# Attention scores of two heads as two 64-row matmuls of 128 queries, in a new order of steps

## The chip, the core and the metric

The program runs on one core of a Trainium2 chip. The number that counts is the device time of one execution in microseconds (us), as a median of several runs. TensorE is called PE here (PEld is its weight load), VectorE DVE, ScalarE ACT, GpSimd POOL, and SyncE, which issues most of the DMAs, SP.

## What is computed

The program does three things one after the other: attention with a causal mask and a bias from a running sum, a mixture of eight experts, and a gated layer. Only the attention is touched:

```python
batch, n_heads, seq, head_dim = (4, 8, 576, 64)
scores = scale * np.matmul(q, k.transpose(0, 1, 3, 2))
s_pos = np.maximum(s, 0.0)
cum = np.cumsum(s_pos, axis=-1)
bias = -(cum[:, :, :, None] - cum[:, :, None, :])
scores = np.where(causal, -1000000000.0, scores + np.minimum(bias, 0.0))
scores = scores - np.max(scores, axis=-1, keepdims=True)
attn = np.exp(scores)
attn = attn / (np.sum(attn, axis=-1, keepdims=True) + 1e-09)
return np.matmul(attn, v).astype(np.float32)
```

Since every row's maximum is subtracted, a constant per row falls out, so only the running sum of the keys has to be added to the scores.

## The kernel before

The 32 heads are worked on as 16 pairs p = 0..15; a pair's two heads lie in partitions 0 to 63 and 64 to 127 of q, k and v. One pair goes through these steps:

- `attn_load`, `load_bias`, `load_v` (L212 to L238): DMAs of q, k, the running sum from a scratch tensor `cumd`, broadcast over 64 partitions per head, and v. `q_diag` (L241, POOL) spreads q into nine block-diagonal tiles `bd` of 128 x 128: head 0's 64 queries in one quarter, head 1's in the opposite one, zeros elsewhere.
- `s_mm` i = 0..8 (L255): 64 queries of both heads against w = 64(i+1) keys, one matmul over all 128 rows (L266), then a bf16 matmul over the last 64 columns that adds the mask (L268). DVE adds the running sum and takes the row's minimum (L269) into one of three `sc` buffers. i = 8 is done in two halves of 288 columns.
- `s_exp` i = 0..8 (L276): ACT takes the exponential and sums it up (L279). `s_norm` (L283): DVE gathers the sums of both heads and takes reciprocals.
- `t_mm` g = 0..6 (L295): 25 transposes of 128 x 128, four to a PSUM bank (L302), each bank copied by ACT (L304).
- `pv_mm` j = 0..4 (L307): attention times v; the two heads write partitions 0 to 63 and 64 to 127 of one bank (L318, L322). `pv_out` (ACT) copies out.
- `o_mm` i = 0..4 (L333): transposes back with the router's weights appended (L346); DVE scales by the reciprocals (L350, L353).
- After every fourth pair `route` (L370) picks the experts in a chain of small DVE steps with one group of matmuls in it (L409 to L413), and scatters rows to memory.

An f32 matmul is two MATMUL instructions (two passes) with a weight load each. On PE, ACT and DVE the order is the program's: `attention` (L524) adds every step to a list at 10p + a position from the table `POS` and sorts, so that steps of several pairs interleave; T of one pair runs among S of the next, for example. POOL's order and that of the DMA issues on SP are the framework's. PSUM has eight banks, which all of these steps take in turn.

At the start `cumulate` (L127) makes the running sum on DVE, writes it to `cumd`, and for pair 0 alone spreads it over partitions with matmuls (L145).

Of the kernel before, what the change touches and what calls it, by code (L numbers as in the profile page):

```python
# [89 lines left out]
def masks(k):  # L90
    nc, P = k.nc, k.apool
    k.identb = P.tile([128, 128], BF16, name="identb")
    nc.vector.tensor_copy(k.identb, k.ident)
    mk = slot(k, 8, [128], name="mk")
    k.maskm = P.tile([128, 64], BF16, name="maskm")
# [3 lines left out]
    nc.vector.tensor_copy(k.maskm[0:64, :], mk[0:64, 0:64])  # L99
    nc.vector.tensor_copy(k.maskm[64:128, :], mk[64:128, 64:128])  # L100


# [24 lines left out]
def cumulate(k):  # L127
    nc = k.nc
    w = slot(k, 7, [3 * S + NBIAS], name="cumw")[0:32, :]
    s, z, c, d = w[:, 0:S], w[:, S:2 * S], w[:, 2 * S:3 * S], w[:, 3 * S:]  # L130
# [8 lines left out]
    both = k.apool.tile([32, 128], F32, name="both")  # L139
    nc.vector.tensor_copy(both.rearrange("p (h n) -> p h n", h=2),  # L140
                          k.ident[0:32, 0:2].unsqueeze(2).broadcast_to((32, 2, 64)))
    yield
    for n, (a, b) in enumerate(((0, 256), (256, 768), (768, 1280), (1280, 1344))):
        ps = k.psum.tile([128, 512], F32, name=f"cb{n}", tag="b")
        nc.tensor.matmul(ps[:, 0:b - a], both, d[:, a:b], start=True, stop=True)  # L145
        nc.scalar.copy(k.st[0].bias[:, a:b], ps[:, 0:b - a])
        yield

# [24 lines left out]
NBIAS = 1344  # L173
BASE = (0, 0, 0, 0, 256, 256, 256, 256, 768)
NT64 = S // 64
PB = (0, 1, 2, 4, 6, 9, 12, 16, 20)
JB = (0, 9, 16, 21, 24)
NBLK = 25
BLOCKS = [(j, i) for j in range(5) for i in range(2 * j, NT64)]
HALF = S // 2  # L180


def attn_statics(k):
    nc, A = k.nc, k.apool
    k.inp, k.p, k.pvt = [], [], []
    for n in range(2):
        w = slot(k, 4 + n, [3648], name=f"in{n}")
        bd = w[:, 2496:3648].rearrange("p (i n) -> p i n", n=128)
        nc.gpsimd.memset(bd[0:64, :, 64:128], 0.0)
        nc.gpsimd.memset(bd[64:128, :, 0:64], 0.0)  # L190
        k.inp.append((w[:, 0:576], w[:, 576:1152], w[:, 1152:2496], bd))
        if n == 0:
            attn_load(k, 0)
    w = slot(k, 3, [3200], name="vp")
    k.vv = [w[:, 640 * n:640 * n + 640].rearrange("p (h j d) -> p h j d", h=2, j=5) for n in range(3)]
    k.pvt = [w[:, 1920 + 640 * n:2560 + 640 * n] for n in range(2)]
    for n in range(2):
        nc.gpsimd.memset(k.pvt[n][:, S:640], 0.0)
        p = slot(k, n, [NBLK * 128], name=f"p{n}")
        for i in range(0, NT64, 2):  # L200
            nc.gpsimd.memset(p[:, 128 * PB[i] + 64 * (i + 1):128 * PB[i] + 64 * (i + 2)], 0.0)
        k.p.append(p)
    k.pt = slot(k, 2, [NBLK * 128], name="pt")
# [89 lines left out]


def t_mm(k, p, g):  # L295
    nc = k.nc
    src = k.p[p % 2]
    ps = k.psum.tile([128, 512], F32, name=f"t{p}_{g}", tag="b")
    blocks = BLOCKS[4 * g:4 * g + 4]
    for n, (j, i) in enumerate(blocks):  # L300
        a = 128 * (PB[i] + j)
        nc.tensor.transpose(ps[:, 128 * n:128 * n + 128], src[:, a:a + 128], k.ident)  # L302
    w = 128 * len(blocks)
    nc.scalar.copy(k.pt[:, 512 * g:512 * g + w], ps[:, 0:w])  # L304


def pv_mm(k, p, j):  # L307
    nc = k.nc
    st = k.st[p]
    pt = k.pt.rearrange("p (b h n) -> p b h n", h=2, n=64)  # L310
# [141 lines left out]
def order_experts(k):  # L452
# [71 lines left out]
def attention(k):  # L524
    k.st, k.todo = {}, []
    with ExitStack() as es:
# [23 lines left out]
        for p in range(NP):  # L550
# [707 lines left out]
def block_kernel(ctx, tc, q, kk, v, s, w_gate, w1, w2, wg, wv, wo, rms_g, out):  # L1258
# [8 lines left out]
    k.cumd = k.dpool.tile([32, NBIAS], F32, name="cumd")  # L1267
# [80 lines left out]
```

## Time and profile before

| | |
|---|---|
| median of 3 runs | 947.14 us (945.52 to 948.28) |
| the profiled execution | 944.19 us, of which 942.5 us is the span from first to last instruction |
| PE busy | 904.4 us (96%), 5560 matmul instructions |
| DVE / ACT / POOL busy | 463.1 / 407.7 / 346.3 us |

Matmuls overlap in their pipeline, so a matmul's own duration is longer than the step from its start to the next one's start; what a matmul costs PE is that step. The shares of the whole span are means over very different stages; the attention lies in about the first 224 us.

### The profile page before, as it was taken

How to read it: one execution, taken by the hardware profiler on the slowest of the kernel's cores; microseconds unless marked ns; L12 is line 12 of the kernel's file. 1: busy time of each engine (PE TensorE's matmuls, PEld its weight loads, DVE VectorE, ACT ScalarE, POOL GpSimd, SP SyncE). 2: the span in 40 equal slices, each digit the busy share in tenths (PEclk: the TensorE clock that was granted, in tenths of full speed). 3: DMA queues.
4: the chain of work that ended last, by engine and by line, in shares of the span. 5: the costliest groups of instructions: out<-in, count | busy, mean ns of one | idle time of the engine just before them, and what ended most of it. 6: DMA issues, size and time to landing. Idle time of an engine off the chain costs nothing.

```text
span 942.5 us, 15470 instructions
## 1 busy us (share of the span) xinstructions
PE 904.4 (96%) x5560; PEld 800.5 (85%) x5560; DVE 463.1 (49%) x1368; ACT 407.7 (43%) x963; POOL 346.3 (37%) x324
## 2 busy tenths in 40 slices
PE   6999999999979999999899999999999998899995
PEld 3677777678869999999899999999999995688884
DVE  4556565555442555335795444555444699800000
ACT  3777777776546565566351111111111222333310
POOL 4102333124447666767111011110011146697541
PEclk9999999999989999999999999999999999999998
DMA  6986675431637656565731111101111122110000
GB/s 203 276 248 177 165 215 165 110 101 51 211 117 219 208 186 176 185 190 163 244 111 45 46 45 45 45 26 43 46 45 45 46 90 90 47 68 34 34 34 37
DMA packets 47658, 109.13 MB, mean 116 GB/s; under 512 B 6688, under 2 KB 14395, under 8 KB 47571
## 3 DMA queue, kind: packets, MB, share of 16 engines
q1 hardware_dynamic: 44611, 98.42, 35.0%
q0 software_dynamic: 2912, 9.46, 2.6%
q8 instruction: 45, 0.74, 0.3%
q14 instruction: 42, 0.34, 0.1%
q10 hardware_dynamic: 48, 0.17, 0.0%
HBM read 87.17 MB, written 20.86 MB: 115 GB/s over the span
## 4 chain that ended last, share of the span: by engine, by line
PE 83%; DVE 8%; issue 4%; POOL 2%; ACT 1%; POOLq 0%; ACTq 0%; DVEq 0%
PE gg L1028 32%; PE g L750 11%; PE s L266 9%; PE g L734 8%; PE go L1053 8%; PE pvy L318 5%; PE t L302 4%; PE tl L346 3%; DVE raw L981 2%; DVE raw L971 1%; PE xp L705 1%; PE r L799 1%; ACT raw L975 1%; PE r L788 1%; PE cb L145 1%
## 5 line engine op out<-in xcount | busy, mean ns | idle before, releaser
L1028 PE MATMUL gg<-gx,ws 128*128 128x384 f32 x1728 | 300.4, 335 | 0.0
L1028 PEld LDWEIGHTS gg<-gx,ws 128*128 128x128 f32 x1728 | 299.6, 188 | 0.1
L618 POOL TENSOR_TENSOR u<-raw,u 128x1024 fp32r<-128x1024 f32 x64 | 153.9, 2418 | 105.8 <-ACT u L617 102.1
L984 POOL TENSOR_TENSOR ws<-raw,ws 128x256 fp32r<-128x256 f32 x48 | 36.7, 785 | 257.5 <-DVE ws L983 250.3
L269 DVE CUSTOM_DVE_ANT_0 sc<-s,in 128x288 f32<-128x288 f32 (+8 forms) x160 | 70.5, 452 | 85.6 <-PE s L268 78.9
L750 PE MATMUL g<-h,u 128*128 128x256 f32 (+7 forms) x768 | 107.3, 298 | 4.5 <-DVE h L738 3.3
L750 PEld LDWEIGHTS g<-h,u 128*128 128x128 f32 x768 | 102.9, 191 | 5.6 <-DVE h L738 3.7
L266 PE MATMUL s<-in 128*128 128x288 f32 (+8 forms) x320 | 105.2, 429 | 0.1
L734 PE MATMUL g<-xt,u 128*128 128x256 f32 (+7 forms) x768 | 104.2, 295 | 0.0
L734 PEld LDWEIGHTS g<-xt,u 128*128 128x128 f32 x768 | 101.4, 188 | 0.8
L1034 ACT ACTIVATE gh<-gg 128x384 f32<-128x384 f32 x72 | 35.3, 491 | 152.5 <-PE gg L1028 152.5
L279 ACT ACTIVATE p<-sc,nm 128x64 f32<-128x64 f32 (+2 forms) x144 | 81.0, 563 | 14.5 <-DVE nm L272 8.1
L975 ACT ACTIVATE raw<-raw 128x256 f32<-128x256 f32 x72 | 28.0, 440 | 124.4 <-DVE raw L973 117.3
L1035 DVE TENSOR_TENSOR gh<-gg,gh 128x384 f32<-128x384 f32 x72 | 39.9, 555 | 74.5 <-ACT gh L1034 74.5
L617 ACT CAST u<-raw 128x1024 fp32r<-128x1024 f32 x64 | 67.0, 1047 | 4.2 <-DMA raw<-in_w 4.2
L304 ACT COPY pt<-t 128x512 f32<-128x512 f32 (+1 forms) x112 | 59.6, 536 | 19.2 <-PE t L302 18.6
L243 POOL COPY in<-in 64x576 f32<-64x576 f32 x30 | 20.2, 673 | 117.4 <-PE s L268 50.6
L302 PE MATMUL t<-ident,p 128*128 128x128 f32 x400 | 63.1, 276 | 0.0
L1036 DVE TENSOR_TENSOR gh<-gg,gh 128x384 f32<-128x384 f32 x72 | 40.2, 558 | 44.8 <-PE gg L1028 41.3
L758 DVE TENSOR_TENSOR sq<-sq,sn 128x256 f32<-128x256 f32 (+7 forms) x24 | 15.5, 646 | 87.4 <-ACT sn L757 87.4
L266 PEld LDWEIGHTS s<-in 128*128 128x128 f32 x320 | 50.6, 196 | 5.0 <-issue 0.8
L302 PEld LDWEIGHTS t<-ident,p 128*128 128x128 f32 x400 | 46.3, 141 | 2.3 <-DVE nm L269 0.5
(227 smaller groups left out, 1211.7 us busy)
## 6 DMA issues: line engine op xcount, KB each, us to landing
raw<-in_w SPq DMA_DIRECT2D x64, 512.0 KB
in<-cumd SPq DMA_DIRECT2D x30, 336.0 KB
xs<-zrow SPq DMA_DIRECT2D x8, 771.0 KB
raw<-in_wg SPq DMA_DIRECT2D x24, 256.0 KB
raw<-in_wv SPq DMA_DIRECT2D x24, 256.0 KB
raw<-in_wo SPq DMA_DIRECT2D x24, 256.0 KB
vp<-in_v SPq DMA_DIRECT2D x16, 320.0 KB
in<-in_k SPq DMA_DIRECT2D x16, 288.0 KB
```

The source lines that it names most:

```text
L266: nc.tensor.matmul(ps, st.bd[:, i, :], st.k[:, a:b], start=True, stop=not last)
L269: nc.vector.tensor_tensor_reduce(out=sc[:, a:b], in0=ps, in1=st.bias[:, BASE[i] + a:BASE[i] + b], scale=-0.125, scalar=3e38, op0=ALU.add, ...
L279: k.nc.scalar.activation(k.p[p % 2][:, 128 * PB[i]:128 * PB[i] + w], st.p[i][:, 0:w], AF.Exp, bias=st.nm[:, i:i + 1], scale=-1.0, accum_ou ...
L302: nc.tensor.transpose(ps[:, 128 * n:128 * n + 128], src[:, a:a + 128], k.ident)
L304: nc.scalar.copy(k.pt[:, 512 * g:512 * g + w], ps[:, 0:w])
L318: nc.tensor.matmul(st.y[r, 64 * (i - 1):512], st.v[:, h, j, :], pt[:, b:b + NT64 - i, h, :], start=j == 0, stop=j == 4)
L617: nc.scalar.copy(w[:, :, 0, :], raw)
L618: nc.gpsimd.tensor_tensor(w[:, :, 1, :], raw, w[:, :, 0, :].bitcast(F32), op=ALU.subtract)
L734: nc.tensor.matmul(ps[:, 0:n], w[:, f % 4, a, 128 * kc:128 * kc + 128], x[b][:, kc, 0:n], start=kc == 0 and i == 0, stop=kc == 3 and i == 2)
L750: nc.tensor.matmul(ps[:, 0:n], w[:, f % 4, a, 128 * c:128 * c + 128], k.h[b][:, f, 0:n], start=f == 0 and i == 0, stop=f == 7 and i == 2)
L1028: nc.tensor.matmul(ps, w[:, m, a, 128 * kc:128 * kc + 128], b[:, kc, :], start=kc == 0 and n == 0, stop=kc == 3 and n == 2)
L1053: k.nc.tensor.matmul(acc[g][t], c[:, a, cols], w[:, b, :], start=f == 0 and i == 0, stop=f == 11 and i == 2)
```

## The change

- Scores: for i = 0..3 a tile holds 128 queries of one head against w = 128(i+1) keys. The two heads are two matmuls that each use 64 rows (partitions 0 to 63, 64 to 127) and write two banks; q is used as loaded. The mask comes from two bf16 matmuls per head, also of 64 rows (`pick`, `mask`). The last 64 queries of both heads (i = 4) stay one block-diagonal tile of 128 rows.
- There are still nine exponentials, ten DVE reductions and 25 transposes per pair, of other widths; the transposes are grouped otherwise, and the copies of a pair are 10 rather than 7. `sc` has four buffers rather than three.
- The running sum is one per head over all keys, not three re-based ones; it is loaded as `cb` (both heads, over 128 partitions) and `cm` (the layout of before, for the last tile) in four DMAs rather than two. For pair 0, only the first 256 columns are spread by matmuls, and the rest comes by DMA.
- `POS`, the start of `route` and the first of the moments in `EARLY_AT` are new: scores of a pair stand together early in its period of 10, `o_mm` comes later.

```diff
 def cumulate(k):
...
-    nc.vector.tensor_copy(d[:, 0:256], c[:, 0:256])
-    nc.vector.tensor_scalar(d[:, 256:768], c[:, 0:512], c[:, 256:257], None, op0=ALU.subtract)
-    nc.vector.tensor_scalar(d[:, 768:1344], c, c[:, 512:513], None, op0=ALU.subtract)
+    nc.vector.tensor_scalar(d, c, c[:, HALF:HALF + 1], None, op0=ALU.subtract)
     k.cumdone = nc.scalar.dma_start(out=k.cumd, in_=d).ins
...
+    for h in range(2):
+        ps = k.psum.tile([128, 512], F32, name=f"cb{h}", tag="b")
+        nc.tensor.matmul(ps[:, 0:256], k.ident[0:32, h:h + 1].broadcast_to((32, 128)), d[:, 0:256], start=True, stop=True)
+        nc.scalar.copy(k.st[0].cb[:, h, 0:256], ps[:, 0:256])
+    load_bias(k, 0)
...
 def load_bias(k, p):
+    st = k.st[p]
+    c = 256 if p == 0 else 0
     for h in range(2):
-        k.nc.sync.dma_start(out=k.st[p].bias[64 * h:64 * h + 64, :],
-                            in_=k.cumd[2 * p + h:2 * p + h + 1, :].broadcast_to((64, NBIAS)))
+        k.nc.sync.dma_start(out=st.cb[:, h, c:512], in_=k.cumd[2 * p + h:2 * p + h + 1, c:512].broadcast_to((128, 512 - c)))
+    for h in range(2):
+        k.nc.sync.dma_start(out=st.cm[64 * h:64 * h + 64, :], in_=k.cumd[2 * p + h:2 * p + h + 1, :].broadcast_to((64, S)))
...
 def s_mm(k, p, i):
...
-        nc.tensor.matmul(ps, st.bd[:, i, :], st.k[:, a:b], start=True, stop=not last)
-        if last:
-            nc.tensor.matmul(ps[:, b - a - 64:b - a], k.identb, k.maskm, start=False, stop=True)
...
+    if i < 4:
+        w = 128 * (i + 1)
+        rows = (slice(0, 64), slice(64, 128))
+        ps = [k.psum.tile([128, 512], F32, name=f"s{p}_{i}_{h}", tag="b")[:, 0:w] for h in range(2)]
+        for h, r in enumerate(rows):
+            nc.tensor.matmul(ps[h], st.q[r, 128 * i:128 * i + 128], st.k[r, 0:w], start=True, stop=False)
+        for n in range(2):
+            for h, r in enumerate(rows):
+                nc.tensor.matmul(ps[h][:, w - 128 + 64 * n:w], k.pick[r, n, :], k.mask[r, n, 64 * n:128],
+                                 start=False, stop=n == 1)
+        for h in range(2):
+            sc = st.s[i, h] = A.tile([128, S], F32, name=f"sc{p}_{i}_{h}", tag="sc", bufs=4)
+            reduced(k, sc[:, 0:w], ps[h], st.cb[:, h, 0:w], st.nm[:, 2 * i + h:2 * i + h + 1])
+    else:
+        sc = st.s[4, 0] = A.tile([128, S], F32, name=f"scm{p}", tag="sc", bufs=4)
+        for n in range(2):
+            c = slice(HALF * n, HALF * n + HALF)
+            ps = k.psum.tile([128, 512], F32, name=f"sm{p}_{n}", tag="b")[:, 0:HALF]
+            nc.tensor.matmul(ps, st.bd, st.k[:, c], start=True, stop=n == 0)
+            if n == 1:
+                nc.tensor.matmul(ps[:, HALF - 64:HALF], k.identb, k.mask[:, 0, 0:64], start=False, stop=True)
+            reduced(k, sc[:, c], ps, st.cm[:, c], st.nm[:, 8 + n:9 + n])
...
 def t_mm(k, p, g):
...
+    if g < 2:
+        for i in range(4):
+            tr(128 * i, ph[i][g], 0)
+        ev.append((ps, k.pt[:, g, 0:512]))
+    elif g < 4:
+        for i in range(1, 4):
+            tr(128 * (i - 1), ph[i][g - 2], 1)
+        ev.append((ps[:, 0:384], k.pt[:, g - 2, JB[1]:JB[1] + 384]))
...
 POS = dict(
-    S=[0.0, 0.4, 1.2, 2.1, 3.2, 4.3, 5.4, 6.4, 7.4],
-    X=[1.1, 1.3, 2.2, 3.1, 4.2, 5.3, 6.4, 7.5, 8.6],
-    T=[10.8, 11.6, 12.6, 13.7, 14.8, 15.9, 16.9],
-    V=[18.0, 18.2, 18.4, 18.6, 18.8],
-    W=[19.0, 19.5],
-    O=[22.3, 23.4, 24.5, 25.6, 26.7],
+    S=[0.1, 1.05, 1.3, 1.39, 1.59],
+    X=[0.52, 0.62, 1.15, 1.26, 1.54, 3.21, 4.61, 6.44, 7.19],
+    T=[8.55, 8.8, 9.97, 10.31, 10.73, 11.18, 11.59],
+    V=[13.45, 13.61, 14.86, 15.34, 15.77],
+    W=[15.4, 17.83],
+    O=[25.26, 28.74, 29.95, 31.71, 33.37],
     N=[11.0],
     Q=[-4.0, -3.9],
     Z=[-8.0, -7.9, -7.8],
 )
-ROUTE = (27.0, 0.3)
+ROUTE = (33.6, 0.2)
...
-EARLY_AT = (151.5, 163.5, 168.9, 169.4)
+EARLY_AT = (152.2, 164.0, 168.9, 169.4)
```

## Rows read from the trace of the kernel before

**Rows 1.** Stretches of one pair each: us, busy us of each engine, clock, DMA

```profile
39.30:52.10 12.80, 12.80 (x91) 9.13 (x90) 6.55 (x34) 9.40 (x27) 1.33 (x2) 1.00 0.96 297
77.60:90.40 12.80, 12.80 (x99) 9.13 (x98) 8.73 (x49) 9.50 (x28) 2.48 (x3) 1.00 0.49 128
```

**Rows 2.** Waits from 78 to 206 us: us in total, times, longest

```profile
DVE sc L269 <- PE s L268: 44.5, 40, 2.6
```

**Rows 3.** Timeline of PE in one pair: start, us, merged instructions

```profile
92.13 1.02 PE L266 MATMUL s<-in 128*128 128x512 f32 x2
92.99 0.19 PE L268 MATMUL s<-maskm,identb 128*128 128x64 bf16 x1
93.02 0.49 PE L346 MATMUL tl<-tg,vp 128*128 128x144 f32 x2
...
93.46 1.14 PE L266 MATMUL s<-in 128*128 128x288 f32 x4
94.43 0.19 PE L268 MATMUL s<-maskm,identb 128*128 128x64 bf16 x1
94.55 1.08 PE L318 MATMUL pvy<-pt,vp 128*64 128x512 f32 x4
95.46 0.28 PE L322 MATMUL pvx<-pt,vp 128*64 128x64 f32 x4
...
97.41 0.43 PE L266 MATMUL s<-in 128*128 128x64 f32 x2
...
99.80 0.49 PE L346 MATMUL tl<-tg,vp 128*128 128x144 f32 x2
100.13 0.60 PE L302 MATMUL t<-ident,p 128*128 128x128 f32 x4
100.57 0.70 PE L266 MATMUL s<-in 128*128 128x320 f32 x2
```

**Rows 4.** Timeline of PE from 94.4 to 94.7 us alone

```profile
94.55 0.65 PE L318 MATMUL pvy<-pt,vp 128*64 128x512 f32 x2
```

**Rows 5.** Groups by line and shape, 0 to 420 us: busy us, mean ns

```profile
L304 ACT COPY pt<-t 128x512 f32<-128x512 f32 x96 | 55.4, 580 | 18.9 <-PE t L302 18.6 <-ACT p L279 0.2
L279 ACT ACTIVATE p<-sc,nm 128x576 f32<-128x576 f32 x16 | 12.4, 774 | 8.2 <-DVE nm L272 8.1
L279 ACT ACTIVATE p<-sc,nm 128x64 f32<-128x64 f32 x16 | 5.6, 352 | 0.7 <-DVE nm L269 0.7
L304 ACT COPY pt<-t 128x128 f32<-128x128 f32 x16 | 4.3, 268 | 0.3
```

**Rows 6.** Timeline of the first 31 us, all engines

```profile
3.62 0.65 DVE L99 CAST maskm<-mk 64x64 bf16<-64x64 f32 x1 [1.92 <-POOL mk L97]
4.92 0.84 DVE L133 TENSOR_SCALAR cumw<-cumw 32x576 f32<-32x576 f32 x1
8.32 0.36 ACTq L138 DMA_DIRECT2D cumd<-cumw  x1
14.38 0.78 PE L266 MATMUL s<-in 128*128 128x128 f32 x2
14.47 1.12 SPq L230 DMA_DIRECT2D in<-cumd  x2
22.11 0.41 PE L266 MATMUL s<-in 128*128 128x64 f32 x2
22.39 0.47 PE L266 MATMUL s<-in 128*128 128x128 f32 x2
```

**Rows 7.** Timeline of PE around the last pair's end

```profile
200.61 0.43 PE L266 MATMUL s<-in 128*128 128x64 f32 x2
...
214.30 0.41 PE L346 MATMUL tl<-tg,vp 128*128 128x144 f32 x2
214.54 0.60 PE L302 MATMUL t<-ident,p 128*128 128x128 f32 x4
...
224.25 3.07 PE L734 MATMUL g<-xt,u 128*128 128x256 f32 x24
```

More of the change, by code (lines that the diff above doesn't have):

```diff
@@ L94, in masks @@
     mk = slot(k, 8, [128], name="mk")
-    k.maskm = P.tile([128, 64], BF16, name="maskm")
     nc.gpsimd.memset(mk, 0.0)
@@ L98, in masks @@
                             pattern=[[-1, 128]], channel_multiplier=1)
-    nc.vector.tensor_copy(k.maskm[0:64, :], mk[0:64, 0:64])
-    nc.vector.tensor_copy(k.maskm[64:128, :], mk[64:128, 64:128])
+    k.pick = P.tile([128, 2, 128], BF16, name="pick")
+    k.mask = P.tile([128, 2, 128], BF16, name="mask")
+    nc.gpsimd.memset(k.pick, 0.0)
+    nc.gpsimd.memset(k.mask, 0.0)
+    for h in range(2):
+        r = slice(64 * h, 64 * h + 64)
+        for n in range(2):
+            c = slice(64 * n, 64 * n + 64)
+            nc.vector.tensor_copy(k.pick[r, n, c], k.ident[c, c])
+            nc.vector.tensor_copy(k.mask[r, n, 64 * n:128], mk[c, 64 * n:128])
 def rank_consts(k):
@@ L128, in cumulate @@
     nc = k.nc
-    w = slot(k, 7, [3 * S + NBIAS], name="cumw")[0:32, :]
-    s, z, c, d = w[:, 0:S], w[:, S:2 * S], w[:, 2 * S:3 * S], w[:, 3 * S:]
+    w = slot(k, 7, [4 * S], name="cumw")[0:32, :]
+    s, z, c, d = (w[:, S * n:S * n + S] for n in range(4))
     nc.sync.dma_start(out=s, in_=k.s)
@@ L134, in cumulate @@
     nc.vector.tensor_tensor_scan(c, z, z, 0.0, op0=ALU.add, op1=ALU.bypass)
-    nc.vector.tensor_copy(d[:, 0:256], c[:, 0:256])
-    nc.vector.tensor_scalar(d[:, 256:768], c[:, 0:512], c[:, 256:257], None, op0=ALU.subtract)
-    nc.vector.tensor_scalar(d[:, 768:1344], c, c[:, 512:513], None, op0=ALU.subtract)
+    nc.vector.tensor_scalar(d, c, c[:, HALF:HALF + 1], None, op0=ALU.subtract)
     k.cumdone = nc.scalar.dma_start(out=k.cumd, in_=d).ins
-    both = k.apool.tile([32, 128], F32, name="both")
-    nc.vector.tensor_copy(both.rearrange("p (h n) -> p h n", h=2),
-                          k.ident[0:32, 0:2].unsqueeze(2).broadcast_to((32, 2, 64)))
     yield
[L143 to L147, printed above, removed]
+    for h in range(2):
[3 more added lines that the diff above has]
+    load_bias(k, 0)
+    yield
 FILLS = E
@@ L170, in prefill @@
     after(k, i.ins, [k.cumdone])
[L173 to L179, printed above, removed]
 HALF = S // 2
+PTW = 1600
+JB = (0, 576, 1024, 1344, 1536)
 def attn_statics(k):
     nc, A = k.nc, k.apool
-    k.inp, k.p, k.pvt = [], [], []
+    k.inp, k.p = [], []
     for n in range(2):
[L187 to L191, printed above, removed]
+        w = slot(k, 4 + n, [2880], name=f"in{n}")
+        bd = w[:, 2752:2880]
+        nc.gpsimd.memset(bd[0:64, 64:128], 0.0)
+        nc.gpsimd.memset(bd[64:128, 0:64], 0.0)
+        k.inp.append((w[:, 0:576], w[:, 576:1152], w[:, 1152:2176].rearrange("p (h n) -> p h n", h=2), w[:, 2176:2752], bd))
         if n == 0:
@@ L198, in attn_statics @@
         nc.gpsimd.memset(k.pvt[n][:, S:640], 0.0)
[L199 to L203, printed above, removed]
+        p = slot(k, n, [3200], name=f"p{n}")
+        nc.gpsimd.memset(p[:, 2560 + S:3200], 0.0)
+        q = [[p[:, 1280 * h + 64 * i * (i + 1):1280 * h + 64 * (i + 1) * (i + 2)] for h in range(2)] for i in range(4)]
+        k.p.append((q, p[:, 2560:3200]))
+    k.pt = slot(k, 2, [2, PTW], name="pt")
     k.sm, k.rs = [], []
     for n in range(2):
-        k.sm.append(A.tile([128, NT64], F32, name=f"sm{n}"))
+        k.sm.append(A.tile([128, 1], F32, name=f"sm{n}"))
         t = A.tile([128, 5, 2], F32, name=f"rs{n}")
@@ L242, in q_diag @@
     st, r = k.st[p], slice(64 * h, 64 * h + 64)
-    k.nc.gpsimd.tensor_copy(st.bd[r, :, r], st.q[r, :].rearrange("p (i n) -> p i n", n=64))
+    k.nc.gpsimd.tensor_copy(st.bd[r, r], st.q[r, 512:576])
 def copy(k, eng, out, in_):
@@ L252, in copy, with reduced @@
         k.nc.vector.tensor_copy(out, in_)
+def reduced(k, out, ps, bias, accum):
+    k.nc.vector.tensor_tensor_reduce(out=out, in0=ps, in1=bias, scale=-0.125, scalar=3e38,
+                                     op0=ALU.add, op1=ALU.min, accum_out=accum)
 def s_mm(k, p, i):
@@ L283, in s_norm, with s_exp @@
+def s_exp(k, p, n):
+    st, (ph, pm) = k.st[p], k.p[p % 2]
+    i, h = divmod(n, 2)
+    w = 128 * (i + 1) if i < 4 else S
+    out = ph[i][h] if i < 4 else pm[:, 0:S]
+    acc = k.rs[p % 2][:, i, h:h + 1] if i < 4 else k.sm[p % 2]
+    k.nc.scalar.activation(out, st.s[i, h][:, 0:w], AF.Exp, bias=st.nm[:, n:n + 1], scale=-1.0, accum_out=acc)
 def s_norm(k, p):
@@ L296, in t_mm, with tr, both @@
     nc = k.nc
-    src = k.p[p % 2]
+    ph, pm = k.p[p % 2]
     ps = k.psum.tile([128, 512], F32, name=f"t{p}_{g}", tag="b")
[L299 to L304, printed above, removed]
+    def tr(off, src, j):
+        nc.tensor.transpose(ps[:, off:off + 128], src[:, 128 * j:128 * j + 128], k.ident)
+    def both(a, j, n):
+        return ps[:, a:a + 128 * j].rearrange("p (h n) -> p h n", h=2), k.pt[:, :, n:n + 64 * j]
+    ev = []
+    if g < 2:
[6 more added lines that the diff above has]
+        ev.append((ps[:, 0:384], k.pt[:, g - 2, JB[1]:JB[1] + 384]))
+    elif g == 4:
+        for h in range(2):
+            for i in range(2, 4):
+                tr(256 * h + 128 * (i - 2), ph[i][h], 2)
+        ev.append(both(0, 4, JB[2]))
+    elif g == 5:
+        for h in range(2):
+            tr(128 * h, ph[3][h], 3)
+        for j in range(2):
+            tr(256 + 128 * j, pm, j)
+        ev.append(both(0, 2, JB[3]))
+        ev.append((ps[:, 256:512].rearrange("p (j h n) -> p h j n", j=2, h=2),
+                   k.pt[:, :, 512:512 + 896].rearrange("p h (j c) -> p h j c", j=2)[:, :, :, 0:64]))
+    else:
+        for j in range(2, 5):
+            tr(128 * (j - 2), pm, j)
+        for j in range(2, 5):
+            ev.append(both(128 * (j - 2), 1, JB[j] + 512 - 128 * j))
+    for a, b in ev:
+        nc.scalar.copy(b, a)
 def pv_mm(k, p, j):
@@ L313, in pv_mm @@
         st.xp = k.psum.tile([128, 64], F32, name=f"pvx{p}", tag="b")
-    i = max(2 * j, 1)
-    b = JB[j] + i - 2 * j
+    a = max(128 * j, 64)
+    o = JB[j] + a - 128 * j
     for h in range(2):
         r = slice(64 * h, 64 * h + 64)
-        nc.tensor.matmul(st.y[r, 64 * (i - 1):512], st.v[:, h, j, :], pt[:, b:b + NT64 - i, h, :], start=j == 0, stop=j == 4)
+        nc.tensor.matmul(st.y[r, a - 64:512], st.v[:, h, j, :], k.pt[:, h, o:o + S - a], start=j == 0, stop=j == 4)
     if j == 0:
@@ L321, in pv_mm @@
             r = slice(64 * h, 64 * h + 64)
-            nc.tensor.matmul(st.xp[r, :], st.v[:, h, 0, :], pt[:, 0, h, :], start=True, stop=True)
+            nc.tensor.matmul(st.xp[r, :], st.v[:, h, 0, :], k.pt[:, h, 0:64], start=True, stop=True)
 def pv_out(k, p, i):
@@ L554, in attention @@
             add(10 * p + POS["N"][0], s_norm, k, p)
-            if p > 0:
-                for h, at in enumerate(POS["Q"]):
-                    add(10 * p + at, q_diag, k, p, h)
+            for h, at in enumerate(POS["Q"]):
+                add(max(10 * p + at, 0.5), q_diag, k, p, h)
             for fn, at in zip((attn_load, load_bias, load_v), POS["Z"]):
@@ L1266, in block_kernel @@
     k.tokd = k.dpool.tile([YCOL], F32, name="tokd")
-    k.cumd = k.dpool.tile([32, NBIAS], F32, name="cumd")
+    k.cumd = k.dpool.tile([32, S], F32, name="cumd")
     k.psum = ctx.enter_context(tc.tile_pool(name="psa", bufs=8, space=bass.MemoryType.PSUM))
```

41 lines of the change are left out of this document (9 added, 32 removed).

## The prediction

> **What bounds the kernel now.** I read the stretches pair by pair first. In [rows 1] the reader sees PE busy for all of a 12.8 us stretch, ACT for 9.4 to 9.5, DVE for 6.6 to 8.7, POOL for under 2.5, with PE's clock granted in full. A busy PE proves little by itself, so the waits come next: in [rows 2] the longest wait of the attention is DVE's for score matmuls, 44.5 us; while PE's row in [rows 1] has no gap to give to anyone. So PE's stream of matmuls sets the pace. Pair 1's scores start at 22.11 us [rows 6] and pair 15's at 200.61 [rows 7]: 178.5 us for 14 periods, 12.75 each. Inside a period the steps from start to start are the price of a matmul [rows 3].
>
> **Prices, from [rows 3] unless said.** Two passes over 512 columns take 0.86 (92.13 to 92.99), 0.00168 a column. A mask matmul of 64 columns takes 0.03 (92.99 to 93.02). Four transposes take 0.44 (100.13 to 100.57), 0.11 each. An output step O takes 0.33 behind a mask (99.80 to 100.13) but 0.24 behind a transpose (214.30 to 214.54, [rows 7]): behind so short a matmul, 0.09 of the next weight load is not covered. V takes 2.86 (94.55 to 97.41). Check on the period of before: scores 2880 columns, 4.84, nine masks 0.27, nine uncovered loads 0.81, 25 transposes 2.75, five O 1.20, V 2.86: 12.73 against the 12.75 measured. The prices hold.
>
> **Do the two heads overlap?** Before, no matmul uses 64 rows beside another, so this is bounded from V, whose heads share the array by columns. There four instructions of 512 columns (two heads, two passes) take 0.91 (94.55 to 95.46), not 4 x 0.43 = 1.7: the heads run together. [rows 4] shows two of the four started by 94.7, long before one pass is through, although the code issues both passes of head 0 before head 1. I take the same for 64-row halves: 1280 columns for both heads, 2.15. The other end is no overlap, 4.30. The Trainium skill says otherwise of the order: "TensorE: Matmul & The Clock Gate", Part 3, The mechanism, has matmuls start and end strictly in program order; by that head 1 would wait for head 0's second pass, three passes in place of two. By that rule, V's four would have taken 1.28, and the trace disagrees; it stays a rival below.
>
> **What a change of shape costs.** From the last mask of full width to V the step is 0.12 (94.43 to 94.55) rather than 0.03: 0.09 in which PE empties itself. With a weight load of 0.09 that nothing covers, one change costs 0.18, there and back 0.36. In the new order, sorted from the table, a period runs S0 T3 T4 S1 T5 S2 S3 T6 S4 O3 O4 V0 V1 V2 O0 V3 V4 T0 O1 T1 O2 T2. S0, S1 and S2-S3 are three visits to the 64-row shape, and V is cut in two by O0: four round trips more than before, 1.44. For the 64-row shape no row of before shows a price; below lies nothing, above twice V's. I take V's, the nearest. The Trainium skill, "TensorEngine Tiling (Array Packing)", Key Properties, says that changing the tiling mode drains PE; the 0.09 agrees for V's shape, and no run here shows it for 64 rows. With the drain the sum is the one below; without it, the fourth rival's.
>
> **The new period.** Transposes 2.75 (still 25), O 1.20 (none stands behind a short mask now), V 2.86, 64-row scores 2.15, their masks 4 x 0.09 = 0.36 (128 and 64 bf16 columns), the last tile S4 as the old i = 8 with its 288-column halves 1.09 (93.46 to 94.55), round trips 1.44: 11.85. Saving 0.90 a period, 12.6 over 14.
>
> **What rides on other engines.** Exponentials: nine again, 256 columns more; from 64 columns 352 ns and 576 columns 774 ns [rows 5], 0.21 us. Copies: six of 580 and one of 268 ns become 3 of 512, 2 of 384, 2 of 256, 3 of 128 columns, by the same rows 4.24 us instead of 3.75. ACT goes from 9.4 to 10.1 a period and stays under PE; I price it at nothing because PE's 11.85 covers it, and below 10.1 no saving on PE can carry. DVE's reductions have 256 columns more, about 0.3, against two small copies saved; it has four us of room. The four broadcasts of a running sum are read two pairs ahead on SP and compete with a DMA share of 0.96 early and 0.49 later; they move 800 KB (128 x 512 and 64 x 576 f32, twice each), not 672 (64 x 1344 twice), and PE has no gap in either stretch of [rows 1]. POOL's q copy shrinks from 576 columns to 64. Going along a period: X6 (needs S3) lies some 7 us in and T0 about 9.6, X7 is behind W0, which waits for V0 at 7.7, and ends near 8.8, before T1 at 10.4. PE's steps meet their inputs with over a microsecond to spare.
>
> **Start.** The sum for pair 0's columns from 256 on now comes through `cumd`. Its write is issued at 8.32, and SP's first read behind it starts at 14.47 [rows 6]. Four issues at 0.56 each (1.12 for two) and the travel, which I take as 2 us between nothing and the 6.15 of `cumd` itself, put pair 0's S2 at about 17, three reductions and exponentials later T0 at 19.5, and eleven transposes at half speed (0.22) make pair 1 start at 22.0, as before. Early matmuls are slow: the same instruction pair takes 0.78 at 14.38 and 0.47 at 22.39. PE now pauses before 19.5, so I add 3 us at half speed: -1.5. From -5 (the broadcasts and DVE's eight small mask copies late) to +3 (a smaller `cumd` lands sooner).
>
> **Route.** Its matmuls stand behind V3, two O's worth after the DVE work that they need: O4's scaling waits behind S4's reductions, then seven steps. I charge 1 us in each of three periods: -3 (0 to -6). Its last scatters, now at 151.6, still lie 12 positions before the first step that needs them, at 164.0.
>
> **End.** From pair 15's S0 to the experts' first matmul it is 23.6 us now [rows 7]. After: one period, 11.85, 14 transposes 1.54, twelve O 2.88, V with its cut 3.22, eight transposes of x 0.88, and 0.5 for a wait: 20.9. The scores stand at the head of the last period rather than spread over it: +2.7. Two O's that period 2 no longer holds: +0.5. What follows moves as a block, since it reads rows of the attention and its first weights were split long before.
>
> **The sum.** 12.6 + 0.5 - 1.5 + 2.7 - 3 = 11.3. The profiled execution took 944.2, so it would take 932.9; the median of the runs is 2.9 higher, so I forecast 935.8, rounded 936.
>
> **Rivals.**
> - *The heads don't overlap.* 2.15 and 0.36 more a period: 14.36, that is 1.61 x 14 = 22.5 slower, and the other terms (-1.3) make it 971. For it: no row shows 64-row matmuls side by side. Against: V does it by columns. It decides for slower once more than 0.8 us of those 2.5 fail to overlap.
> - *Head 1 waits for head 0's second pass.* Half of 2.15 more: 12.93, 2.5 slower, with -1.3: 951. [rows 4] speaks against.
> - *A chain of waits takes PE's place*: S0 to S4 stand close together, four `sc` buffers must go through DVE and ACT in turn, and W0 holds up X7. With 0.5 us of PE waiting per period: 12.35, 5.6 less, 4.3 in all: 943. For it: ACT at 10.1 is fuller than before.
> - *The 64-row shape changes for nothing.* Three round trips less, 10.77: 27.7 - 1.3: 921. ACT's 10.1 leaves room for it.
>
> **Chances.** Forecast 0.56 (its own range 929 to 942, from a round trip between 0.25 and 0.45 and the start's ends), chain 0.16, free changes 0.12, order of passes 0.06, no overlap 0.07, something else 0.03. From 920 to 951 holds all but the third of the free case that goes lower, no overlap, and the rest. A measurement tells 0.3% (2.8 us) from no change: faster 0.56 + 0.12 + 0.13 of the chain = 0.81; within it 0.06; slower 0.13.
>
> **What would show it.** Right: score matmuls of the two heads starting within some 10 ns of each other; a tile of 512 columns and its masks within about 1 us; periods near 11.85 and PE still without gaps; 0.09 at each change of shape; pair 1 starting near 22; the experts' first matmul near 213. Wrong: second-head matmuls starting a pass later, PE idle before T0, V0 or the route's matmuls, or a late `cumd` that pushes pair 1 beyond 25.

## The result, and the profile after

The changed kernel takes 934.35 us (median of 4 runs, 934.07 to 934.51) against 946.33 us of the kernel before, run beside it (4 runs, 944.86 to 948.28): a ratio of 0.9872 [0.9852, 0.9892], 1.3% faster. The prediction was 936 in a range from 920 to 951. The same kernel, run again in a later set of four runs (e9 below), takes 928.62 us (928.46 to 928.85; 0.9816 [0.98, 0.9832]). Within each set the runs agree to 0.5 us, so what parts the two is not the chance of one execution; what it is (the chip, or how the program lay there) isn't shown. One execution of each set is traced. They are called the first and the second execution from here on and are kept apart: 934.07 us, of which 932.3 is the span, and a span of 927.0. One of e7's four runs below took 1088.5 us at a granted clock of 0.75; it is left out of e7's ratio.

The windows of the changed kernel, for two undisturbed pairs and for the pair behind the first route (from the start of a pair's first scores to the next pair's; columns as in [rows 1]):

```profile
40.63:52.65 12.02, 12.02 (x97) 8.00 (x96) 6.31 (x30) 9.78 (x31) 0.47 (x2) 1.00 1.08 281
52.65:64.68 12.03, 12.03 (x97) 8.01 (x97) 6.32 (x30) 9.79 (x31) 0.47 (x2) 1.00 1.04 298
89.22:102.11 12.89, 12.18 (x97) 8.00 (x96) 6.24 (x30) 9.39 (x31) 4.98 (x7) 1.00 0.59 192
```

PE is still busy without a gap in the first two, so it still sets the pace, with a period (the time from one pair's first scores to the next pair's) of 12.03 in place of 12.76. ACT has gone from 9.4 [rows 1] to 9.8, DVE has room. In the third row PE stands for 0.71 of 12.89.

The timeline of PE in the second of these pairs, to be read beside [rows 3]; what counts is the step from one start to the next:

```profile
52.65 0.49 PE L261 MATMUL s<-in 64*128 64x128 f32 x4
52.98 0.25 PE L264 MATMUL s<-mask,pick 64*128 64x128 bf16 x4
53.16 0.98 PE L306 MATMUL t<-ident,p 128*128 128x128 f32 x7
54.07 0.70 PE L261 MATMUL s<-in 64*128 64x256 f32 x4
...
56.21 1.11 PE L261 MATMUL s<-in 64*128 64x512 f32 x4
57.15 0.25 PE L264 MATMUL s<-mask,pick 64*128 64x128 bf16 x4
57.34 0.55 PE L306 MATMUL t<-ident,p 128*128 128x128 f32 x3
57.72 1.14 PE L274 MATMUL sm<-in 128*128 128x288 f32 x4
58.69 0.19 PE L276 MATMUL sm<-mask,identb 128*128 128x64 bf16 x1
58.72 0.74 PE L380 MATMUL tl<-tg,vp 128*128 128x144 f32 x4
59.39 1.08 PE L352 MATMUL pvy<-pt,vp 128*64 128x512 f32 x4
...
61.80 0.51 PE L380 MATMUL tl<-tg,vp 128*128 128x144 f32 x2
62.25 0.66 PE L352 MATMUL pvy<-pt,vp 128*64 128x192 f32 x8
62.84 0.65 PE L306 MATMUL t<-ident,p 128*128 128x128 f32 x4
```

The tile of 512 columns needs 0.94 for both heads together (56.21 to 57.15), where one 512-column tile of full width took 0.86 [rows 3]. A view that ends 50 ns after the start of the first score matmul shows how:

```profile
52.65 0.38 PE L261 MATMUL s<-in 64*128 64x128 f32 x2
```

Two of the four instructions have started by then, and the trace gives their starts as 52.654 and 52.661, the other two as 52.868 and 52.874: head 1's first pass starts 7 ns behind head 0's, though the code issues both passes of head 0 first (in e1 below, where both heads use the same rows, the four run one behind the other, and the semaphore updates of the two heads stand on the second and the fourth; here, in the 512-column tile, on the third and the fourth). The Trainium skill, "TensorE: Matmul & The Clock Gate", Part 3, The mechanism, has matmuls start and end in program order; for two halves of the array this trace disagrees.

The start, over all engines, beside [rows 6]:

```profile
7.54 0.35 ACTq L141 DMA_DIRECT2D cumd<-cumw  x1
7.66 2.04 PE L145 MATMUL cb<-cumw,ident 32*128 32x256 f32 x4 [7.66 <-DVE cumw L140]
11.54 0.81 SPq L220 DMA_DIRECT2D in<-cumd  x2
14.58 0.56 DVE L247 CUSTOM_DVE_ANT_0 sc<-s,in 128x384 f32<-128x384 f32 x1 [2.02 <-DMA in<-cumd]
17.51 1.36 PE L306 MATMUL t<-ident,p 128*128 128x128 f32 x8 [1.24 <-ACT p L287]
18.80 0.49 PE L261 MATMUL s<-in 64*128 64x128 f32 x4
```

The first read of `cumd` starts 4.0 us behind the write's issue; before it was 6.15 [rows 6]. Pair 1 starts at 18.80, not at 22.11.

**Where the time went.** Us gained against the kernel before, from the traces; "again" is the second execution. Pair 1's scores start at 22.11 before, 18.80 and 18.51 after; pair 15's at 200.61, 188.76 and 186.16; the experts' first matmul at 224.25, 211.86 and 207.88; the spans end at 942.5, 932.3 and 927.0.

| | predicted | first | again |
|---|---|---|---|
| start, to pair 1 | -1.5 | +3.3 | +3.6 |
| 14 periods, 12.76 to 12.03 | 12.6 | 10.2 | 10.2 |
| O's missing in the first periods | +0.5 | +0.7 | +0.7 |
| routes and the pairs behind them | -3 | -2.4 | -0.1 |
| end, pair 15 to the experts | +2.7 | +0.5 | +1.9 |
| all that follows | 0 | -2.2 | -0.9 |
| sum | 11.3 | 10.1 | 15.4 |

The forecast was close to the first execution because errors of both signs met: 2.4 less from the periods, 4.8 more from the start, and 5.3 us that the second execution doesn't lose. That 934 stands so near 936 is in part luck; the second set lies 7 from the forecast, inside its range.

### The profile page after: what moved, and what is told of

The parts are those of the page before. It is cut to its first block, busy times and chain, and to the rows that moved or that the text cites. A ratio compares the mean times of both kernels' runs of the same rounds, so it can differ in the third digit from the quotient of the medians.

```text
span 932.3 us, 15830 instructions
## 1 busy us (share of the span) xinstructions
PE 889.3 (95%) x5684; PEld 781.1 (84%) x5684; DVE 460.2 (49%) x1339; ACT 410.8 (44%) x1009; POOL 332.9 (36%) x320
## 4 chain that ended last, share of the span: by engine, by line
PE 84%; DVE 6%; issue 4%; POOL 3%; ACT 2%; DMA 1%; POOLq 0%; DVEq 0%; ACTq 0%
PE gg L1061 32%; PE g L783 11%; PE g L767 8%; PE go L1086 8%; PE t L306 6%; PE pvy L352 5%; PE s L261 5%; PE tl L380 3%; PE sm L274 2%; DVE raw L1014 1%; DVE raw L1004 1%; PE xp L738 1%; PE r L832 1%; POOL gx5b L1077 1%; PE r L821 1%
## 5 line engine op out<-in xcount | busy, mean ns | idle before, releaser
L287 ACT ACTIVATE p<-sc,nm 128x128 f32<-128x128 f32 (+3 forms) x128 | 72.4, 572 | 12.0 <-DVE nm L247 8.3
L247 DVE CUSTOM_DVE_ANT_0 sc<-s,in 128x128 f32<-128x128 f32 (+3 forms) x128 | 57.5, 489 | 39.0 <-PE s L264 19.9
L339 ACT COPY pt<-t 128x512 f32<-128x512 f32 (+3 forms) x160 | 62.2, 433 | 11.6 <-PE t L306 7.4
L352 PE MATMUL pvy<-pt,vp 128*64 128x512 f32 (+4 forms) x320 | 50.8, 433 | 1.5 <-ACT pt L339 0.8
L261 PE MATMUL s<-in 64*128 64x128 f32 (+3 forms) x256 | 51.5, 491 | 0.0
L306 PEld LDWEIGHTS t<-ident,p 128*128 128x128 f32 x400 | 43.8, 141 | 6.9 <-ACT p L287 2.2
L234 POOL COPY in<-in 64x64 f32<-64x64 f32 x32 | 8.0, 251 | 116.0 <-DMA in<-in_q 106.0
## 6 DMA issues: line engine op xcount, KB each, us to landing
xs<-zrow SPq DMA_DIRECT2D x8, 771.0 KB, 10.2
```

The source lines that it names most:

```text
L247: k.nc.vector.tensor_tensor_reduce(out=out, in0=ps, in1=bias, scale=-0.125, scalar=3e38, op0=ALU.add, op1=ALU.min, accum_out=accum)
L261: nc.tensor.matmul(ps[h], st.q[r, 128 * i:128 * i + 128], st.k[r, 0:w], start=True, stop=False)
L287: k.nc.scalar.activation(out, st.s[i, h][:, 0:w], AF.Exp, bias=st.nm[:, n:n + 1], scale=-1.0, accum_out=acc)
L306: nc.tensor.transpose(ps[:, off:off + 128], src[:, 128 * j:128 * j + 128], k.ident)
L339: nc.scalar.copy(b, a)
L352: nc.tensor.matmul(st.y[r, a - 64:512], st.v[:, h, j, :], k.pt[:, h, o:o + S - a], start=j == 0, stop=j == 4)
```

## The experiments

Each was timed beside the kernel before; the four columns are the time, the ratio, the undisturbed period and the start of pair 1. Numbers in the text are from these and from the traces.

| | us | ratio | period | pair 1 |
|---|---|---|---|---|
| changed kernel, first | 934.35 | 0.9872 [0.9852, 0.9892] | 12.03 | 18.80 |
| e9, the same again | 928.62 | 0.9816 [0.98, 0.9832] | 12.03 | 18.51 |
| e1, one half of the array | 971.97 | 1.0281 [1.0257, 1.0306] | 14.51 | 24.05 |
| e2, old order of steps | 927.03 | 0.9804 [0.9782, 0.9826] | 11.86 | 16.06 |
| e3, old tiles, new order | 950.2 | 1.0051 [1.0036, 1.0066] | 13.09 | 25.42 |
| e4, V not cut | 924.93 | 0.9782 [0.976, 0.9805] | 11.73 | 18.40 |
| e5, two visits | 925.6 | 0.9794 [0.9778, 0.9811] | 11.76 | 19.47 |
| e6, four visits | 934.63 | 0.9888 [0.9872, 0.9905] | 12.34 | 18.24 |
| e7, one visit, V not cut | 916.59 | 0.9698 [0.9679, 0.9718] | 11.19 | 19.75 |
| e8, wide running sum | 929.68 | 0.9833 [0.9817, 0.985] | 12.03 | 19.06 |
| e10, route half a unit later | 927.9 | 0.9809 [0.9792, 0.9825] | 12.03 | 18.49 |
| e11, q again in small pieces | 931.57 | 0.9853 [0.9837, 0.987] | 12.03 | 20.12 |

**e1: do the halves overlap?** Both heads' 64-row matmuls use partitions 0 to 63, so head 1's scores are head 0's.

```diff
-        rows = (slice(0, 64), slice(64, 128))
+        rows = (slice(0, 64), slice(0, 64))
```

> Both heads' 64-row score and mask matmuls take partitions 0 to 63, so that the two heads use the same half of the array; head 1's scores are then head 0's, nothing else is changed. Theory (the gain is that the two halves run together): each pair pays for 1280 columns and the masks twice, 2.15 + 0.36 us more, so the period goes from 12.03 to about 14.5 and the time from 934.4 to about 972 us. Rival (the new order and the shorter start made the gain, and the overlap is hidden behind other engines): within 5 us of 934.

PE's timeline of the tile of 512 columns:

```profile
70.45 1.96 PE L261 MATMUL s<-in 64*128 64x512 f32 x4
72.25 0.33 PE L264 MATMUL s<-mask,pick 64*128 64x128 bf16 x4
```

1.80 instead of 0.94, a period of 14.51 instead of 12.03, 972 us: with the overlap taken away, the kernel comes out near the first rival's 14.36 and 971. All of the gain of the new tiles, and more, is the overlap.

**e2 and e3: tiles and order apart.** e2 keeps the new tiles and goes back to the old table (its S and X at the new tiles' places); e3 keeps the old tiles with four `sc` buffers and takes the new table. The core of e2:

```diff
-    S=[0.1, 1.05, 1.3, 1.39, 1.59],
-    T=[8.55, 8.8, 9.97, 10.31, 10.73, 11.18, 11.59],
-    V=[13.45, 13.61, 14.86, 15.34, 15.77],
-    O=[25.26, 28.74, 29.95, 31.71, 33.37],
-ROUTE = (33.6, 0.2)
+    S=[0.4, 2.1, 4.3, 6.4, 7.4],
+    T=[10.8, 11.6, 12.6, 13.7, 14.8, 15.9, 16.9],
+    V=[18.0, 18.2, 18.4, 18.6, 18.8],
+    O=[22.3, 23.4, 24.5, 25.6, 26.7],
+ROUTE = (27.0, 0.3)
```

> The new tiles with the old table: the five score tiles are spread over the period, V is not cut, route and the early loads are where they were. Four round trips of shape for the scores rather than three and none for the cut of V: same PE work. Theory (tiles bring the steady gain, the order only the last pair's end): period about 12.0, end of the attention 2 to 3 us later than with the new order, 936 to 938 us. Rival (the tiles need the new order, otherwise PE waits): period 12.5 or more, 942 us or more.

> The old tiles (64 queries of both heads, 128 rows) in the new order, two tiles at each new place, with four buffers for scores. Theory: PE has the work of before plus one more round trip of shape for the cut of V, 0.36, and fewer exposed places for O: period 12.6 to 13.1, time 944 to 951 us. Rival (the order is what helps): 940 us or less.

The tiles alone do it: 11.86 a period in the old order. The new order alone makes the old tiles slower, 13.09 against 12.76, which is near the price of V's cut that e4 finds. With the new tiles it saves one visit to the 64-row shape (a stretch of matmuls in that shape with others before and behind it) and pays V's cut for it, and comes out 0.17 a period behind the old order. The traces show where most of that lies: in e2, S0 stands right behind V (V4 at 63.03, S0 at 63.24), so that leaving V's shape and entering the 64-row one are a single change. In the changed kernel transposes stand between, and those behind V and before S0 take 0.06 and 0.09 more than others. Of the end, e3 takes 21.86 from pair 15 to the experts and e2 23.55, before 23.64: the end's gain is the order's. Behind it the new order loses: from the experts' first matmul to the end e2 takes 718.24, before 718.23, e9 719.09. (e3's 720.19, like the first execution's 720.41, holds 1.6 us of another kind, shown at the end of the next section.)

**e4: V's cut.** O0 of an earlier pair goes behind V instead of into it.

```diff
-    O=[25.26, 28.74, 29.95, 31.71, 33.37],
+    O=[25.9, 28.74, 29.95, 31.71, 33.37],
```

> O0 moved behind V4, so that V is not cut and one round trip of shape per period goes; nothing else is changed. Theory (a round trip costs 0.36): 15 to 16 times 0.36, 5 to 6 us faster than the changed kernel, 929 us, if no wait comes in. Rival (O0 in V hides a wait for V's last blocks or the shape change is covered): within 1 us of 934.4.

The period falls by 0.30, to 11.73; e3's rise of 0.33, in which more than the cut has changed, is near it. The total fell by 9.4 against the first execution, more than fifteen times 0.30; against e9's 928.62 it is 3.7, so the surplus lay in the execution that it was compared with.

**e5 and e6: the price of a visit.** S0 moves to S1 (a visit fewer), or S3 behind T6 (a visit more).

```diff
 # e5
-    S=[0.1, 1.05, 1.3, 1.39, 1.59],
-    X=[0.52, 0.62, 1.15, 1.26, 1.54, 3.21, 4.61, 6.44, 7.19],
+    S=[1.04, 1.05, 1.3, 1.39, 1.59],
+    X=[1.06, 1.07, 1.15, 1.26, 1.54, 3.21, 4.61, 6.44, 7.19],
 # e6
-    S=[0.1, 1.05, 1.3, 1.39, 1.59],
+    S=[0.1, 1.05, 1.3, 1.6, 1.61],
```

> S0 moved to stand directly before S1: two visits to the 64-row shape per pair instead of three, nothing else. Theory (each visit costs PE one round trip, 0.30 to 0.36 us): period 12.03 to about 11.7, 15 periods give 4.5 to 5.4 us, total near 929.5. Rival (with four sc buffers S0 and S1 together leave PE waiting for the reductions and exponentials): period 12.0 or more, a wait of PE at S2 in the waits, total 934 or more.

> S3 moved behind T6, so S2 and S3 are two visits: four visits per pair instead of three. Theory: period 12.03 plus 0.30 to 0.36, about 12.36, total near 939.5. Rival (the shape change is free or hidden, and after's period is set by waits instead): period stays within 0.1 of 12.03, total 934.

A period of 11.76 and one of 12.34: -0.27 and +0.31. A visit costs that here, and nothing hides it. e6's total looks like no change against the first execution, but is 6.0 over the second (e6 has a disturbed period and the lower clock of the first execution too, both shown below).

**e7: all in one visit.** e4's table, with S0 to S3 side by side.

```diff
-    S=[0.1, 1.05, 1.3, 1.39, 1.59],
-    X=[0.52, 0.62, 1.15, 1.26, 1.54, 3.21, 4.61, 6.44, 7.19],
-    O=[25.26, 28.74, 29.95, 31.71, 33.37],
+    S=[1.28, 1.29, 1.3, 1.39, 1.59],
+    X=[1.31, 1.32, 1.4, 1.41, 1.54, 3.21, 4.61, 6.44, 7.19],
+    O=[25.9, 28.74, 29.95, 31.71, 33.37],
```

> All four 64-row tiles stand in one visit, and V isn't cut. By round trips alone: against the run with V whole (11.73) two visits fewer, 0.6 to 0.72, period near 11.05, total near 915. Rival (chain of waits): eight score tiles go through four sc buffers, so S2 has to wait until the exponentials of S0 are through; four exponentials in a row on ACT are about 1.5 us, of which PE waits over 0.6: period 11.7 or more, with PE waits for ACT or DVE at S2 or S3 in every period, total 925 or more.

The windows of one of its periods, and PE's timeline at the visit:

```profile
51.38:62.57 11.19, 11.19 (x97) 8.04 (x96) 6.26 (x29) 9.74 (x31) 0.47 (x2) 1.00 1.04 294
```

```profile
51.07 0.38 PE L306 MATMUL t<-ident,p 128*128 128x128 f32 x2
51.38 0.49 PE L261 MATMUL s<-in 64*128 64x128 f32 x4
51.71 0.25 PE L264 MATMUL s<-mask,pick 64*128 64x128 bf16 x4
51.79 0.68 PE L261 MATMUL s<-in 64*128 64x256 f32 x4
52.31 0.25 PE L264 MATMUL s<-mask,pick 64*128 64x128 bf16 x4
52.39 0.90 PE L261 MATMUL s<-in 64*128 64x384 f32 x4
```

11.19, two visits fewer than e4's three for 0.54, so 0.27 each, and PE without a gap. The expected wait didn't come: the eight score tiles go through four `sc` buffers, but it is DVE that needs these; by the code PE only needs a free PSUM bank. At 916.59 us this is the fastest version, 3.0% below the kernel before; its gain over the changed kernel is that of the visits and of V's cut together. A row also shows what was forgotten in the sum: S1, right behind S0's masks and with no change of shape, takes 0.52 (51.79 to 52.31), where 256 columns were priced at 0.43. The 0.09 is the weight load that the short mask doesn't cover.

**e8 and e11: the start.** e8 writes the running sum 1344 columns wide as before; e11 loads pair 0's q once more in 64-column pieces, as the kernel before does, into memory that nothing reads.

```diff
 # e8
-    w = slot(k, 7, [4 * S], name="cumw")[0:32, :]
+    w = slot(k, 7, [3 * S + 1344], name="cumw")[0:32, :]
...
-    k.cumdone = nc.scalar.dma_start(out=k.cumd, in_=d).ins
+    k.cumdone = nc.scalar.dma_start(out=k.cumw, in_=w[:, 3 * S:]).ins
 # e11, in attn_load
+    if p == 0:
+        for h in range(2):
+            r = slice(64 * h, 64 * h + 64)
+            nc.sync.dma_start(out=k.more[r, :, r], in_=k.q[p][r, :].rearrange("p (i n) -> p i n", n=64))
```

> The running sum is written to memory 1344 columns wide, as before the change, with 576 of them used; all else as after the change. Theory (the earlier start comes from the smaller write, whose readers start 4.0 us behind its issue instead of 6.15): pair 1 starts some 2 us later than 18.80, near 20.9, total near 936.5. Rival (the start is earlier because pair 0 has fewer, wider pieces of work): pair 1 at 18.8, total 934.

> Pair 0's q is loaded once more, in the 64-column pieces of the kernel before, into memory that nothing reads; all else as after the change. Theory (the readers of the running sum start 6.15 us behind its write before the change because the DMA engines were full with such small packets): the reads start 5 to 6 us behind the write instead of 4.0, pair 1 at 20 to 21 in place of 18.8, total up by 1.5 to 2. Rival (the turnaround has another cause, such as the number of loads ahead on SP): reads 4.0 us behind the write, pair 1 within 0.3 of 18.8.

e8's timeline, write and first read:

```profile
8.23 0.36 ACTq L142 DMA_DIRECT2D cumd<-cumw  x1
11.40 0.80 SPq L221 DMA_DIRECT2D in<-cumd  x2
```

e11's, and below it the windows of e9 and of e11 from 8 to 12 us:

```profile
7.45 0.36 ACTq L141 DMA_DIRECT2D cumd<-cumw  x1
12.90 0.81 SPq L225 DMA_DIRECT2D in<-cumd  x2
```

```profile
8.00:12.00 4.00, 4.00 (x22) 2.71 (x23) 0.80 (x5) 1.62 (x6) 0.87 (x5) 1.00 0.57 229
```

```profile
8.00:12.00 4.00, 4.00 (x22) 2.69 (x23) 0.82 (x5) 1.62 (x6) 1.37 (x7) 1.00 0.91 358
```

The size of the write is not the reason, and that theory falls: the wide one is read 3.2 us behind its issue (and is issued 0.7 later, behind a longer setup on POOL and DVE). The loads of q are: with the extra ones the reads start 5.45 us behind the write, the DMA share from 8 to 12 us is 0.91 in place of 0.57, and pair 1 starts 1.6 later. That is 1.4 of the 2.1 us between 4.0 and 6.15; where the other 0.7 lies is open. SP's own issues are not what takes longer: in e9 it waits 6.8 us for the write and in e11 6.7, with no other issue in between. But e11 adds 288 KB and two issues as well as small pieces, and the same bytes in wide pieces were not tried, so that it is the size of the pieces is not shown.

**e9 and e10: the idle stretches of the first execution.** e9 is the changed kernel unaltered. (The pairs 8 and 12 of its expectation are 7 and 11 when counted from 0.) e10 moves the route's steps.

```diff
-ROUTE = (33.6, 0.2)
+ROUTE = (34.1, 0.2)
-EARLY_AT = (152.2, 164.0, 168.9, 169.4)
+EARLY_AT = (152.7, 164.0, 168.9, 169.4)
```

> The changed kernel as it is, once more, because its steady part (169.96 us from pair 1 to pair 15) is 2.3 us longer and its tail (23.10) 1.4 longer than those of the run with the wide running sum (167.65 and 21.71), which differ in nothing there. Theory (the stretches in which DVE stands idle behind the scores of pair 8 and pair 12 belong to this program): 934, periods of 12.89 and 13.47 again. Rival (they belong to that execution or chip, not to the program): periods 12.03 throughout, near 929.

> The 40 steps of a route start half a position table unit later (34.1 in place of 33.6), so that the scatters on POOL stand elsewhere against the scores of the pair that follows. Theory (the idle stretches of DVE come from where the scatters fall): the periods 12.89 and 13.47 change, towards 12.03, or up by as much; total between 929 and 937. Rival (the scatters have nothing to do with it): as the changed kernel run beside it, within 1 us.

DVE's timeline behind the first route, in the first execution:

```profile
90.81 0.22 DVE L297 RECIPROCAL r<-r 128x10 f32<-128x10 f32 x1
93.11 0.42 DVE L247 CUSTOM_DVE_ANT_0 sc<-s,in 128x256 f32<-128x256 f32 x1 [2.09 <-PE s L264]
...
96.20 0.56 DVE L247 CUSTOM_DVE_ANT_0 sc<-s,in 128x384 f32<-128x384 f32 x1 [2.31 <-PE tl L380]
```

and in e9:

```profile
90.52 0.22 DVE L297 RECIPROCAL r<-r 128x10 f32<-128x10 f32 x1
91.18 0.42 DVE L247 CUSTOM_DVE_ANT_0 sc<-s,in 128x256 f32<-128x256 f32 x1 [0.44 <-PE s L264]
...
92.80 0.56 DVE L247 CUSTOM_DVE_ANT_0 sc<-s,in 128x384 f32<-128x384 f32 x1 [0.85 <-PE s L264]
```

The same reduction starts 0.29 behind the start of its tile's mask matmuls in e9 (90.89 to 91.18) and 1.93 in the first execution (91.18 to 93.11). In e9 the periods are 12.03 throughout (12.52 in a route pair), so the stretches of 12.89 and 13.47, and a third like them in the tail, belong to the execution or chip, not to the program: the rival of e9's expectation holds. (e6 has one such period too, 12.92.) e10's question is void with that; it shows another thing, that steps of a route half a unit later cost 0.25 instead of 0.49 in its pair, 0.7 in all. Why the first execution was disturbed stays open. Its trace records PE's semaphore updates at 91.59, 93.09, 94.57 and 96.07, 1.5 us apart, and DVE's two late starts are 0.02 to 0.13 behind two of these. But it holds only 8 of PE's updates in the 6.9 us from the pair's start where e9's holds 19, so the spacing may be only that of what was recorded. POOL issues indirect DMAs from 88.78 to 94.95, but in e9 as well.

## Why the prediction was right, and where not

**The mechanism** holds as it was put. PE's stream sets the pace before and after; the heads overlap (7 ns between their starts, and e1, where they can't, takes the first rival's time); ACT at 9.8 and DVE at 6.3 fit under a period of 12.03; no chain of waits took PE's place, even with all scores in one visit. The order-of-passes rival would have made the 512-column tile three passes, 1.28; it took 0.94. Free changes of shape, the fourth rival, are out by e5 to e7.

**The period**, 12.03 instead of 11.85, is the term whose size was off. Four round trips were priced at 0.36. Measured, a visit to 64 rows is 0.27 to 0.31 and V's cut 0.30 to 0.33. The Trainium skill's "TensorEngine Tiling (Array Packing)", Key Properties, says that PE drains when the mode changes, and these agree. So the four are some 1.15 (1.11 to 1.26) and not 1.44. Two things were left out against that. The sum for the kernel before counted nine weight loads behind short masks, 0.09 each; the sum for the changed one counted none for its four 64-row tiles, though each stands behind a mask or a change of shape (0.09 x 4, as e7's row shows). And O3 does stand behind a short mask, that of S4, though the prediction says that none does: O3 and O4 take 0.67 (58.72 to 59.39) where 0.48 was priced. Half of that 0.19 is only moved: the step into V's shape, which was priced in S4's 1.09, now falls on O4, and S4 took 1.00 (57.72 to 58.72). -0.29 + 0.36 + 0.19 - 0.09 is 0.17 of the missing 0.18; the 2.4 us that the steady part gave less than the 12.6 forecast are 14 of these. With the clean differences alone (0.27 three times and 0.30) it would be 0.13. The rest may be the step out of V's shape, which neither sum has: O0 right behind V takes 0.35 in e4 (61.24 to 61.59), behind a transpose 0.25.

**The start** failed at one step: that SP's first read of `cumd` starts at 14.47 as before. It starts at 11.54, because the write is issued 0.8 earlier and read 2.1 sooner behind its issue; 1.4 of these 2.1 go again when q is loaded once more in small pieces (e11). From there the steps held: S2's reduction 3.0 later (2.5 forecast), the transposes 2.9 later (2.5), pair 1 1.3 later (2.5). Three of the eleven transposes had run before 17.51, and they were not slow: PE's steps are down to their later size from S3 on (two heads of 512 columns 0.94 from 13.02 on, as at 56.21). So the 3 us of half speed cost nothing that shows; PE waited for the sums and the exponentials, 1.24 us before 17.51 alone.

**The routes** were charged 1 us each beyond what they cost before. A pair with a route takes 0.49 more than an undisturbed one, three of them 1.5; before, the three and what followed them took 1.4 more than undisturbed pairs. So the new order loses next to nothing here, where 3 was forecast; the -2.4 of the first execution is the disturbance.

**The end** gave 1.9 of 2.7 in e9, 0.5 in the first execution, which lost 1.4 in a third idle stretch of DVE there. **What follows** was taken to move as a block. It lost 0.9 in e9. A wait of PE at the experts' first matmuls is part of it, 2.7 in the first execution and 2.2 in e9:

```profile
PE g L783 <- DVE h L771: 2.7, 1, 2.7
```

```profile
PE g L783 <- DVE h L771: 2.2, 1, 2.2
```

Before, and in e2's old order, this wait is 1.8 and 1.7: in the new order the last O's and the last route stand closer to the experts. In e9 PE also waits 0.25 for the last route's picks, at 211.04, which before it doesn't; e2's order shows neither. The rest is open. In the first execution the granted clock falls to the lower of its levels, 1.2 GHz, from 449.80 to 453.20, after PE had stood idle for 1.3 and for 1.5 us. The row of the windows:

```profile
449.80:453.20 3.40, 3.40 (x18) 3.40 (x18) 1.42 (x4) 1.36 (x3) 0.12 (x1) 0.50 0.59 163
```

In e9 PE stands idle for the same 1.3 and 1.5 us there, and the clock doesn't fall. The 86 matmuls behind the second wait tell what that is worth, first execution and e9:

```profile
448.96 11.74 PE L783 MATMUL g<-h,u 128*128 128x248 f32 x86 [1.50 <-DVE h L771]
```

```profile
445.26 10.16 PE L783 MATMUL g<-h,u 128*128 128x248 f32 x86 [1.50 <-DVE h L771]
```

So 1.6 us of what the first execution has more behind the attention is this, and other waits give 0.3 of it back. The traces of e1, e3, e5, e6 and e8 have it too, those of the kernel before, e2, e4, e7, e10 and e11 don't; a total of one group against one of the other holds 1.6 us that no edit made. The kernel before and e9 have a stretch of lower clock later, from 814.0 and from 791.9, but it costs nothing that stays: from the gated layer's first matmul to the end these two and the first execution, which has none there, all take 471.6 to 471.7.

## What to carry to other kernels

Two matmuls that each fill half of the array run side by side if they stand next to each other, and the saving is then the columns, less a price for each change of shape (0.3 us here): put all work of one shape together before anything else is tuned, as e7 does for 18 us against the changed kernel's first time, 12 against its second. When a new period is summed up, count in the new order every weight load that a short matmul doesn't cover, as for the old one. And repeat the kernel itself beside the experiments: 5.7 us of the first result did not come with the program the second time, although its four runs agreed to 0.5 us, and every comparison with it alone would have been wrong by that.

## What the runs showed that was not expected

- In one traced execution of a program DVE's reductions behind the scatters of a route start 1.6 to 3.1 us later than in the other, against the pair's first scores; in the profile this looks like an ordinary wait for a matmul.
- Further loads in pieces of 64 columns, issued ahead of a small write, delay it by 1.4 us (5.45 against 4.0 until its reader starts).
- The same matmuls behind the same idle time of 1.3 and 1.5 us run at 1.2 GHz for 3.4 us in six of the traces and at 2.4 GHz in the other seven, 11.5 to 11.6 against 10.0 us until the next stage.
- Behind a 64-row visit the first transpose takes 0.165 and not 0.109, on top of the drain: the trace's starts in the period shown give 0.202 for the step into the shape and 0.120 for the last mask out of it, against 0.109 and 0.022 within one shape.
